# The last stage of an attention, expert and gated-product kernel, put in another order

## The chip, the cores and the metric

The kernel runs on one core of a Trainium2 chip. A core has five engines that run side by side, each through its own list of instructions in order: TensorE (PE in the profile; PEld is its weight load), VectorE (DVE), ScalarE (ACT), GpSimd (POOL) and SyncE (SP), which here only starts DMAs. Matrix products land in PSUM, eight banks of 128 x 512 fp32 numbers; all other data is in SBUF. The metric is the device time of one execution in microseconds: the median of three runs of the kernel before is 660.23 us (657.31 to 660.39).

## The reference

Three stages follow one another. Attention with a local and a global part gives `x` (1536 tokens x 512). Each token then goes to the one expert of eight that a gate picks, `relu(x @ w1[e]) @ w2[e]`, scaled. The last stage is the one that is changed:

```python
def _moe2_ref(x, w_a, w_b, w_out):      # x 1536x512, w_a and w_b 512x1536, w_out 1536x512
    a = x @ w_a
    b = x @ w_b
    return (a * b @ w_out).astype(np.float32)
```

The inputs of the last stage's weights are 64-bit floats, which the kernel turns into 32-bit ones itself.

## The kernel before

**Products in three parts.** A 32-bit number is split into a high part `h` (rounded, type fp32r) and a low part `l = x - h`. Each 128-deep product is three matmuls, high x high, high x low and low x high (`mul`, lines 1104 to 1111, and `out_tile`, lines 1154 to 1173). Every operand therefore costs a cast on ScalarE (`h`) and a subtraction on VectorE or GpSimd (`l`).

**Weights.** `wm` holds 18 tiles of 128 x 1024: numbers 0 to 11 carry, for a block `f` of 128 columns, `w_a` and `w_b`; numbers 12 to 17 carry `w_out`. A half tile `(m, half)` passes through four functions. `cload` (line 847) starts a DMA into one of three buffers `st`. `conv1` is two ScalarE operations, the second in place in `st`. `conv2` is three VectorE operations, clip (line 871), shift (873) and merge (874), and one GpSimd add (876), after which `st` is free. `conv3` is a ScalarE cast (884) and a GpSimd subtraction (885). The result of the add, `tx`, has four buffers.

**Stages.** Eight experts run first (`for k, n in enumerate(CAPS)`, line 917). Each is a first product over eight blocks (`up`) and a second over four (`down`), with background work called from `tick(i)`, i = 0 to 15: 0 to 7 follow the blocks of the first product, 8 to 15 lie in the second. The table `CV` (line 909) sets which conversions ride along. A block `h` of the first product passes ScalarE and VectorE (lines 721 to 726) before the second product can read it. Then comes a conditional block (`tc.If(rare[0] == 1)`, line 979), taken only if an expert has more tokens than planned; with these inputs it is not taken, but every engine passes its branch.

**The last stage.** The tokens are three chunks `c` of 512. For chunk 0 the operands were read and split during the experts (`yT`). For chunks 1 and 2 six DMAs bring them into `acc` behind the branch (line 1246), and `ysp` splits them. Blocks `f` = 0 and 1 are multiplied plainly (`plain`, 48 matmuls for each of the three chunks, lines 1255 to 1262). Blocks 2 to 11 run through `seven(f)`, called a step below: chunks 0 and 1 share seven products instead of eight (`pa`, `pb`, `pc` are its PSUM banks; `T1` to `T4` are sums of weight quarters, made for the next step by `tsum`, four VectorE operations, and split by `tsplit`; `S1` to `S4`, `A11`, `A12`, `A22` are the token side), chunk 2 is multiplied plainly into the banks `ab`. The products `a` and `b` are multiplied and split into `gh` and `gl` (`gate`). After each odd step twelve output tiles (`out_tile`, six matmuls each, three PSUM buffers `o`) become possible; `fill(n)` issues `n` of them. A step holds 66 matmuls and six tiles of six, 102 in all. VectorE adds every tile into `acc` (line 1166).

**What sets the order.** The schedule is written by hand (`tc.manual_schedule()`): each engine runs its instructions in the order in which the calls stand in the code, and semaphores make it wait. So a waiting instruction holds up all that is behind it on its engine.

Of the kernel before, what the change touches and what calls it, by code (L numbers as in the profile page):

```python
# [46 lines left out]
def moe_block_kernel(ctx, tc, qd, kd, vd, kt, vn, nv, wg, wg2, we, wm, out):  # L47
# [819 lines left out]
    def conv2(j):  # L867
        sv, tx = raw64.pop(j), tx32[j]
        h, l, txi = sv[:, :, 1], sv[:, :, 0], tx[:, :].bitcast(I32)

# [446 lines left out]
```

## Time and profile before

| what | value |
|---|---|
| median of three runs | 660.23 us (657.31 to 660.39) |
| profiled execution | 659.8 us, of which the span is 658.1 us |
| TensorE busy | 583.6 us (89%) |
| VectorE busy | 460.0 us (70%) |
| ScalarE busy | 307.1 us (47%) |
| GpSimd busy | 253.5 us (39%) |

The shares are means over stages with different limits. In the last stage the slices of the profile's page show VectorE at 5 to 9 tenths and TensorE between 6 and 9, so the question there is which engine is waited for at each pause of TensorE. Matmuls are pipelined: a 128 x 512 one is shown as 0.39 us long, while the next starts some 0.23 us later, so a stretch is measured from start to start.

### The profile page before, as it was taken

To read this page: it belongs to the slowest core of one execution; us is meant where nothing else is said; L and a number is where in the kernel's file an instruction comes from. 1 tells how busy PE (TensorE), PEld (TensorE's weight loads), DVE (VectorE), ACT (ScalarE), POOL (GpSimd) and SP (SyncE) were. 2 spreads that over 40 slices of the span, in tenths; PEclk is the share of its full clock that TensorE was granted. 3 is DMA by queue.
4 is the path that set the end of the run, shared out by engine and by line. 5 is a ranking of instruction groups with operands and counts; after the bars stand their busy time and mean duration, and the time that the engine had idled before them with its cause. 6 is when DMAs were issued, how large, how long until landed. Compare 5 with 4: busy or idle time off the path is not lost.

```text
span 658.1 us, 9962 instructions
## 1 busy us (share of the span) xinstructions
PE 583.6 (89%) x3395; PEld 491.9 (75%) x3395; DVE 460.0 (70%) x982; ACT 307.1 (47%) x681; POOL 253.5 (39%) x231
## 2 busy tenths in 40 slices
PE   6998994999999998987967998898799799879996
PEld 4786773899999897987745776677587577758784
DVE  6888785877447777771676577695876859587653
ACT  5776772556557766761445333423413332341210
POOL 3001532644354655532225544252433415253215
PEclk9999996899999998998979999899799979989999
DMA  8367515475667977844410112020110202010004
GB/s 284 124 206 278 164 55 166 165 254 197 224 224 228 290 258 219 274 155 139 175 64 32 64 65 85 12 97 30 66 64 33 96 0 97 29 67 0 1 22 170
DMA packets 34431, 85.14 MB, mean 129 GB/s; under 512 B 5792, under 2 KB 12192, under 8 KB 34368
## 3 DMA queue, kind: packets, MB, share of 16 engines
q1 hardware_dynamic: 27456, 71.45, 32.2%
q10 hardware_dynamic: 4752, 6.00, 2.9%
q0 software_dynamic: 2160, 6.91, 2.9%
q8 instruction: 31, 0.51, 0.3%
q14 instruction: 32, 0.26, 0.1%
HBM read 73.25 MB, written 11.10 MB: 128 GB/s over the span
## 4 chain that ended last, share of the span: by engine, by line
DVE 21%; PE 16%; issue 7%; ACT 6%; POOL 2%; POOLq 0%; DVEq 0%; ACTq 0%
DVE tx L873 3%; PE ps_o L1161 3%; PE ps_o L1159 3%; DVE tx L874 3%; PE ps_o L1160 3%; DVE gl L1126 2%; DVE tx L871 2%; DVE tt L1093 2%; ACT tx L862 2%; POOL out L1168 1%; ACT st L864 1%; PE ps_pa L1110 1%; PE ps_pa L1109 1%; PE ps_pa L1111 1%; DVE p L1215 1%
## 5 line engine op out<-in xcount | busy, mean ns | idle before, releaser
L110 POOL TENSOR_TENSOR wl<-st,wh 128x512 fp32r<-128x512 f32 x54 | 70.1, 1319 | 89.6 <-ACT wh L105 80.0
L876 POOL TENSOR_TENSOR tx<-tx,st 128x512 int32<-128x512 int32 x36 | 51.0, 1416 | 125.5 <-DVE tx L874 86.6
L105 ACT CAST wh<-st 128x1024 fp32r<-128x1024 f32 x64 | 67.3, 1054 | 33.0 <-DMA st<-we 32.0
L1159 PE MATMUL ps_o<-wh,gh 128*128 128x512 f32 x144 | 61.6, 427 | 20.6 <-ACT gh L1125 8.9
L885 POOL TENSOR_TENSOR wl<-tx,wh 128x512 fp32r<-128x512 f32 x36 | 50.2, 1408 | 66.2 <-ACT wh L884 66.2
L110 DVE TENSOR_TENSOR wl<-st,wh 128x1024 fp32r<-128x1024 f32 x37 | 52.5, 1418 | 28.7 <-ACT wh L105 28.7
L712 PE MATMUL ps_y<-h,wl 128*128 128x256 f32 (+5 forms) x256 | 69.9, 273 | 0.0
L712 PE MATMUL ps_h<-x,wl 128*128 128x256 f32 (+5 forms) x256 | 69.4, 271 | 0.0
L1161 PE MATMUL ps_o<-wh,gl 128*128 128x512 f32 x144 | 61.4, 426 | 5.7 <-DVE gl L1126 5.7
L1160 PE MATMUL ps_o<-wl,gh 128*128 128x512 f32 x144 | 60.3, 418 | 0.0
L1166 DVE TENSOR_TENSOR acc<-ps_o,acc 128x512 f32<-128x512 f32 x60 | 40.5, 686 | 25.2 <-PE ps_o L1161 24.9
L708 PE MATMUL ps_y<-h,wh 128*128 128x448 f32 (+3 forms) x160 | 53.3, 389 | 4.4 <-DVE h L726 4.1
L511 ACT ACTIVATE pe<-pe,mx 128x256 f32<-128x256 f32 (+1 forms) x96 | 45.9, 481 | 22.0 <-DVE mx L507 22.0
L1159 PEld LDWEIGHTS ps_o<-wh,gh 128*128 128x128 f32 x144 | 29.5, 205 | 32.3 <-ACT gh L1125 10.7
L712 PEld LDWEIGHTS ps_y<-h,wl 128*128 128x128 f32 x256 | 50.2, 196 | 0.0
L712 PEld LDWEIGHTS ps_h<-x,wl 128*128 128x128 f32 x256 | 49.4, 193 | 0.0
L708 PE MATMUL ps_h<-x,wh 128*128 128x448 f32 (+3 forms) x160 | 47.9, 365 | 0.0
L884 ACT CAST wh<-tx 128x512 fp32r<-128x512 f32 x36 | 22.2, 620 | 54.0 <-POOL tx L876 53.7
L1161 PEld LDWEIGHTS ps_o<-wh,gl 128*128 128x128 f32 x144 | 29.4, 204 | 14.6 <-DVE gl L1126 7.4
L507 DVE CUSTOM_DVE_ANT_0 pe<-ps_s,bias 128x256 f32<-128x256 f32 (+1 forms) x96 | 32.8, 398 | 7.7 <-PE ps_s L501 6.6
L708 PEld LDWEIGHTS ps_y<-h,wh 128*128 128x128 f32 x160 | 31.7, 198 | 7.7 <-ACT hs L724 4.5
L1125 ACT CAST gh<-a 128x512 fp32r<-128x512 f32 x16 | 9.9, 620 | 56.8 <-DVE a L1227 42.6
(302 smaller groups left out, 1588.5 us busy)
## 6 DMA issues: line engine op xcount, KB each, us to landing
st<-we SPq DMA_DIRECT2D x63, 512.0 KB, 4.4
st<-wm SPq DMA_DIRECT2D x32, 512.0 KB, 3.4
vc<-vd SPq DMA_DIRECT2D x16, 352.0 KB, 3.9
k<-kd SPq DMA_DIRECT2D x7, 464.0 KB, 5.7
x_dram<-x SPq DMA_DIRECT2D x6, 512.0 KB, 3.8
acc<-y_dram SPq DMA_DIRECT2D x6, 512.0 KB, 6.3
q<-qd SPq DMA_DIRECT2D x7, 384.0 KB, 6.0
st<-wm ACTq DMA_DIRECT2D x4, 512.0 KB, 5.0
```

Source lines behind the costliest of these rows:

```text
L105: A.copy(wh, st)
L110: eng.tensor_tensor(wl[:, r], st[:, r], wh[:, r].bitcast(F32), ALU.subtract)
L507: V.tensor_tensor_reduce(out=pe[:, t_, j, 0:n], in0=ps[:, j, t_, 0:n], in1=bias[2 * p + j][:, b0:b0 + n], op0=ALU.add, op1=ALU.min, scale= ...
L511: A.activation(pe[:, t_, j, 0:n], pe[:, t_, j, 0:n], AF.Exp, bias=mx[:, t_, j:j + 1], scale=-1.0, accum_out=sm[:, t_, j:j + 1])
L708: T.matmul(pt[:, 0:2 * n].rearrange("p (s n) -> p s n", s=2), a, M[:, k], start=(k == 0), stop=False)
L712: T.matmul(pt[:, 0:n], b, M[:, k, 0], start=False, stop=(k == last))
L876: G.tensor_tensor(txi, txi, l, ALU.add)
L885: G.tensor_tensor(wl_, tx, wh.bitcast(F32), ALU.subtract)
L1159: T.matmul(po, gh, wh, start=(i == 0), stop=False)
L1160: T.matmul(po, gh, wl, start=False, stop=False)
L1161: T.matmul(po, gl, wh, start=False, stop=(i == 1))
L1166: V.tensor_tensor(acc[:, m], po, acc[:, m], ALU.add)
```

## The change

Line numbers of the changed kernel differ: lines 871, 873, 874, 876 become 874, 876, 877, 879; lines 884 and 885 become 890 and 891; `tsum` moves to 1115 to 1118, `tsplit`'s subtraction from 1102 to 1125, line 1189 to 1240, lines 1196 and 1197 to 1254 and 1255. The parts:

- `conv2` takes several halves and issues all clips, then all shifts, all merges, all adds.
- In the last expert the conversion of tile 1 moves out of the first product into the second.
- The 48 matmuls of chunk 0 for blocks 0 and 1 (`first`) stand in front of the conditional block, in four PSUM buffers of the experts; the block repeats them at its end if it is taken.
- `a * b` is written over the bank that holds `b` (or the corresponding sum), and `gh` and `gl` are made from PSUM.
- In a step all three conversions of the next weights are issued at its start, their casts and subtractions together later, and the products, tiles and gates are put in another order, different for even and odd `f`.
- The opening of the last stage is reordered, and `fill` takes the chunks in the order 2, 0, 1.

The diff, cut to its core:

```diff
@@ product, up, down: the PSUM buffers they take are now a parameter
+    def product(Ws, M, n, name, top, bg=None, tag=("h", 6)):
...
+        pt = ps.tile([P, 512], F32, tag=tag[0], bufs=tag[1], name=name)
...
@@ conv2: one call for several halves, operation by operation
-    def conv2(j):
-        sv, tx = raw64.pop(j), tx32[j]
-        h, l, txi = sv[:, :, 1], sv[:, :, 0], tx[:, :].bitcast(I32)
-        V.tensor_scalar(tx, tx, LO32, HI32, ALU.max, ALU.min)
-        V.tensor_scalar(txi, txi, 3, 0x3FFFFFF8, ALU.logical_shift_left, ALU.bitwise_and)
-        V.scalar_tensor_tensor(txi, h, -0x40000000, txi, ALU.bitwise_and, ALU.bitwise_or)
-        G.tensor_tensor(txi, txi, l, ALU.add)
+    def conv2(*js):
+        ops = []
+        for j in js:
+            sv, tx = raw64.pop(j), tx32[j]
+            h, l, txi = sv[:, :, 1], sv[:, :, 0], tx[:, :].bitcast(I32)
+            ops.append((
+                lambda tx=tx: V.tensor_scalar(tx, tx, LO32, HI32, ALU.max, ALU.min),
+                lambda t=txi: V.tensor_scalar(t, t, 3, 0x3FFFFFF8, ALU.logical_shift_left, ALU.bitwise_and),
+                lambda t=txi, h=h: V.scalar_tensor_tensor(t, h, -0x40000000, t, ALU.bitwise_and, ALU.bitwise_or),
+                lambda t=txi, l=l: G.tensor_tensor(t, t, l, ALU.add)))
+        for o in zip(*ops):
+            for f in o:
+                f()
@@ the last expert's table of background work
-        (7, 11): [(cload, nc.sync)], (7, 12): [(cload, nc.sync)], (7, 13): [(cload, nc.sync)],
-        (7, 2): [(conv1, (1, 0)), (conv2, (1, 0))], (7, 9): [(conv1, (1, 1)), (conv2, (1, 1))],
+        (7, 8): [(conv1, (1, 0))], (7, 9): [(conv2, (1, 0))], (7, 10): [(conv1, (1, 1))], (7, 11): [(conv2, (1, 1))],
+        (7, 12): [(cload, nc.sync)], (7, 13): [(cload, nc.sync)], (7, 14): [(cload, nc.sync)],
@@ behind the last expert, in front of the conditional block
+    def first():
+        for (f, s_), pt in N0.items():
+            mul(pt, wab(f, s_), yT, True)
     yq.pop(0)()
+    for h in range(2):
+        conv3((1, h))
+    N0 = {(f, s_): ps.tile([P, 512], F32, tag="h", bufs=6, name="ps_n") for f in range(2) for s_ in range(2)}
+    first()
@@ inside the conditional block, at its end (and its up/down take ("x", 2))
+            first()
@@ the gated product is written into PSUM
+    def evict(c, f, pp, h1=(), h2=()):
+        a = tmp("a")
+        A.copy(a, pp[0])
+        run_all(h1)
+        V.tensor_tensor(pp[1], a, pp[1], ALU.mult)
+        low = gate(c, f, pp[1])
+        run_all(h2)
+        low()
...
@@ seven(f), a step; its body is now
+        mul(pa, wab(f, 0, 0, 2), A11, True)
+        A.copy(p1, pa)
+        conv_a()
+        mul(pb, T2, S2, True)
+        V.tensor_tensor(u2, pb, p1, ALU.add)
+        mul(pc, T1, S1, True)
+        mul(pa, wab(f, 0, 2, 4), A12, False, True, True)
+        if f % 2:
+            if jobs:
+                tsum(f + 1)
+            ab2(0)
+        else:
+            fill(2)
+            if jobs:
+                tsum(f + 1)
+            fill(2)
+        conv_b()
+        mul(pb, T3, S3, False, True, True)
+        V.tensor_tensor(u3, pb, p1, ALU.add)
+        V.tensor_tensor(u3, u3, pc, ALU.add)
         if f % 2:
+            low2 = ab2(1)
+            low1 = p4()
+            low2()
+            low0 = p3()
+            low1()
+            low0()
+            for j in nxt:
+                conv1(j)
             both(f // 2)
             fill(6 if f < 11 else 12)
+        else:
+            fill(2)
+            for j in nxt:
+                conv1(j)
+            low1 = p4()
+            low0 = p3()
+            low1()
+            low0()
+            ab2(0)
+            ab2(1)()
     def both(p):
-        items.extend((p, c, t_) for c in (1, 0, 2) for t_ in range(4))
+        items.extend((p, c, t_) for c in (2, 0, 1) for t_ in range(4))
@@ the opening of the last stage
-    plain(0, 0, ("pa", "pb"), [(c12, (12, 0))], [(ysp, X[1, 0], S4, V)])
-    plain(0, 1, ("ab", "ab"), [(ysp, X[1, 1], A22, V)], [(c12, (12, 1)), (conv3, (12, 0))])
...
+    evict(0, 0, (N0[0, 0], N0[0, 1]), [(c12, (12, 0), (12, 1))], [(ysp, X[1, 0], S4, V)])
+    evict(0, 1, (N0[1, 0], N0[1, 1]), [(ysp, X[1, 1], A22, V)], [(conv3, (12, 0)), (ysp, X[2, 0], [y[:, 0:2] for y in Y2], V)])
+    pse.close()
...
+    plain(2, 1, ("pc", "o"), [(ysp, X[1, 1], S1, V), (conv3, (2, 1))], [(ysp, X[1, 0], S3, V), (tsplit, 2)])
+    both(0)
+    fill(2)
+    ysp(X[0, 1], S4, V)
+    c12((13, 0))
+    fill(4)
```

VectorE, in the last expert (`ps_h`, `hs` and `h2` belong to the blocks of the first product, `tx_5120` is a half of tile 1), before:

```order
L725 TENSOR_TENSOR ps_h_5105<-ps_h_5105,hs_5115 128x176
L726 SCALAR_TENSOR_TENSOR h2_5071<-ps_h_5105,h2_5071 128x176
L871 TENSOR_SCALAR tx_5120<-tx_5120 128x512
L873 TENSOR_SCALAR tx_5120<-tx_5120 128x512
L874 SCALAR_TENSOR_TENSOR tx_5120<-st64_4889,tx_5120 128x512
L725 TENSOR_TENSOR ps_h_5127<-ps_h_5127,hs_5137 128x176
L726 SCALAR_TENSOR_TENSOR h2_5071<-ps_h_5127,h2_5071 128x176
L725 TENSOR_TENSOR ps_h_5141<-ps_h_5141,hs_5151 128x176
L726 SCALAR_TENSOR_TENSOR h2_5071<-ps_h_5141,h2_5071 128x176
L725 TENSOR_TENSOR ps_h_5155<-ps_h_5155,hs_5165 128x176
```

and now (`tx_5193` is the same half):

```order
L725 TENSOR_TENSOR ps_h_5162<-ps_h_5162,hs_5172 128x176
L726 SCALAR_TENSOR_TENSOR h2_5071<-ps_h_5162,h2_5071 128x176
L725 TENSOR_TENSOR ps_h_5176<-ps_h_5176,hs_5186 128x176
L726 SCALAR_TENSOR_TENSOR h2_5071<-ps_h_5176,h2_5071 128x176
L874 TENSOR_SCALAR tx_5193<-tx_5193 128x512
L876 TENSOR_SCALAR tx_5193<-tx_5193 128x512
L877 SCALAR_TENSOR_TENSOR tx_5193<-st64_4889,tx_5193 128x512
L734 TENSOR_TENSOR yt_5214<-ps_y_5190,yt_5214 128x176
L874 TENSOR_SCALAR tx_5220<-tx_5220 128x512
L876 TENSOR_SCALAR tx_5220<-tx_5220 128x512
L877 SCALAR_TENSOR_TENSOR tx_5220<-st64_4957,tx_5220 128x512
```

The three conversion operations stood in front of five blocks' operations and now stand behind the last block.

VectorE in the odd step `f` = 5 from the second conversion on (`tx_6710` and `tx_6713` are the halves of tile 6, `tx_6716` one of the output weights, `tt` the sums of `tsum`), before:

```order
L871 TENSOR_SCALAR tx_6713<-tx_6713 128x512
L873 TENSOR_SCALAR tx_6713<-tx_6713 128x512
L874 SCALAR_TENSOR_TENSOR tx_6713<-st64_6560,tx_6713 128x512
L1196 TENSOR_TENSOR u3_6724<-ps_pb_6720,p1_6722 128x512
L1197 TENSOR_TENSOR u3_6724<-u3_6724,ps_pc_6721 128x512
L871 TENSOR_SCALAR tx_6716<-tx_6716 128x512
L873 TENSOR_SCALAR tx_6716<-tx_6716 128x512
L874 SCALAR_TENSOR_TENSOR tx_6716<-st64_6608,tx_6716 128x512
L1092 TENSOR_TENSOR tt_5790<-tx_6713,tx_6710 128x256
L1093 TENSOR_TENSOR tt_5790<-tx_6713,tt_5790 128x256
L1094 TENSOR_TENSOR tt_5790<-tx_6713 128x256
L1095 TENSOR_TENSOR tt_5790<-tx_6710,tt_5790 128x256
```

and now, from the first shift on (the halves are `tx_6700`, `tx_6703` and `tx_6706`):

```order
L876 TENSOR_SCALAR tx_6700<-tx_6700 128x512
L876 TENSOR_SCALAR tx_6703<-tx_6703 128x512
L876 TENSOR_SCALAR tx_6706<-tx_6706 128x512
L877 SCALAR_TENSOR_TENSOR tx_6700<-st64_6602,tx_6700 128x512
L877 SCALAR_TENSOR_TENSOR tx_6703<-st64_6604,tx_6703 128x512
L877 SCALAR_TENSOR_TENSOR tx_6706<-st64_6606,tx_6706 128x512
L1240 TENSOR_TENSOR u2_6769<-ps_pb_6766,p1_6768 128x512
L1115 TENSOR_TENSOR tt_5892<-tx_6703,tx_6700 128x256
L1116 TENSOR_TENSOR tt_5892<-tx_6703,tt_5892 128x256
L1117 TENSOR_TENSOR tt_5892<-tx_6703 128x256
L1118 TENSOR_TENSOR tt_5892<-tx_6700,tt_5892 128x256
L1254 TENSOR_TENSOR u3_6770<-ps_pb_6766,p1_6768 128x512
```

The sums into `u3` stood in front of `tsum` and the third conversion; now they stand behind both.

GpSimd for the same three halves (`wl` are low parts of weights), before:

```order
L876 TENSOR_TENSOR tx_6710<-tx_6710,st64_6554 128x512
L876 TENSOR_TENSOR tx_6713<-tx_6713,st64_6560 128x512
L885 TENSOR_TENSOR wl_6772<-tx_6710,wh_6771 128x512
L885 TENSOR_TENSOR wl_6772<-tx_6713,wh_6771 128x512
L876 TENSOR_TENSOR tx_6716<-tx_6716,st64_6608 128x512
L1102 TENSOR_TENSOR wl_6802<-tt_5790,wh_6801 128x512 x2
L885 TENSOR_TENSOR wl_6850<-tx_6716,wh_6849 128x512
```

and now:

```order
L879 TENSOR_TENSOR tx_6700<-tx_6700,st64_6602 128x512
L879 TENSOR_TENSOR tx_6703<-tx_6703,st64_6604 128x512
L879 TENSOR_TENSOR tx_6706<-tx_6706,st64_6606 128x512
L891 TENSOR_TENSOR wl_6835<-tx_6700,wh_6834 128x512
L891 TENSOR_TENSOR wl_6835<-tx_6703,wh_6834 128x512
L891 TENSOR_TENSOR wl_6841<-tx_6706,wh_6840 128x512
L1125 TENSOR_TENSOR wl_6845<-tt_5892,wh_6844 128x512 x2
```

The third add stood behind two subtractions; now three adds and three subtractions follow one another.

## Rows read from the trace of the kernel before

**Rows 1.** TensorE by stretches: start:end, us, busy (instructions), granted clock, DMA share, GB/s
```profile
291.38:366.62 75.24, 59.26 (x247) 0.89 0.27 90
299.08:304.53 5.45, 5.45 (x42) 1.00 0.78 222
366.62:620.22 253.60, 224.59 (x919) 0.96 0.15 52
620.22:635.30 15.08, 15.08 (x67) 1.00 0.00 0
...
442.40:445.00 2.60, 0.96 (x4) 1.00 0.00 0
466.00:477.00 11.00, 7.35 (x20) 0.69 0.14 49
```

**Rows 2.** Waits of TensorE, steps to the end: engine, line waited for, total, times, longest
```profile
PE ps_o L1159 <- ACT gh L1125: 8.9, 4, 2.2
PE ps_pa L1109 <- ACT p L1187: 7.2, 5, 1.6
PE ps_o L1159 <- DVE acc L1166: 6.5, 4, 1.6
PE ps_o L1161 <- DVE gl L1126: 5.7, 4, 1.4
```

**Rows 3.** Waits of TensorE from the last expert's second product to the first step
```profile
PE ps_pa L1109 <- ACT Y2h L1083: 4.8, 1, 4.8
PE ps_o L1159 <- ACT acc L1164: 4.3, 1, 4.3
PE ps_pa L1109 <- DVEq L979: 3.7, 1, 3.7
PE ps_y L708 <- DVE h L726: 1.8, 2, 1.7
```

**Rows 4.** Timeline, VectorE and GpSimd inside one odd step: start, us, engine, line
```profile
455.64 0.43 DVE L873 TENSOR_SCALAR tx<-tx 128x512 int32<-128x512 int32 x1
...
460.71 2.90 POOL L885 TENSOR_TENSOR wl<-tx,wh 128x512 fp32r<-128x512 f32 x2
...
461.07 1.40 DVE L873 TENSOR_SCALAR tx<-tx 128x512 int32<-128x512 int32 x1
...
462.51 1.66 DVE L874 SCALAR_TENSOR_TENSOR tx<-st,tx 128x512 int32<-128x512 int32 x1
...
467.77 2.53 POOL L1102 TENSOR_TENSOR wl<-tt,wh 128x512 fp32r<-128x512 f32 x2 [2.11 <-ACT wh L1100]
...
467.86 0.68 DVE L1218 TENSOR_TENSOR u<-ps_pc,u 128x512 f32<-128x512 f32 x1
```

**Rows 5.** Groups on VectorE in nine steps: count, busy us, mean ns
```profile
L1126 DVE TENSOR_TENSOR gl<-p,gh 128x512 fp32r<-128x512 f32 x9 | 15.2, 1693 | 0.0
...
L1093 DVE TENSOR_TENSOR tt<-tx,tt 128x256 f32<-128x256 f32 x9 | 12.7, 1411 | 0.3
...
L1126 DVE TENSOR_TENSOR gl<-u,gh 128x512 fp32r<-128x512 f32 x9 | 6.1, 678 | 0.0
...
L1094 DVE TENSOR_TENSOR tt<-tx 128x256 f32<-128x256 f32 x9 | 3.7, 411 | 0.0
```

**Rows 6.** Line 979 (the conditional): ns min/median/max, first and last start
```profile
L979 PEldq EVENT_SEMAPHORE  x2: 51/51/51, 304.7 to 304.9; - x2
...
L979 DVEq EVENT_SEMAPHORE  x2: 21/21/21, 308.2 to 308.3; - x2
```

**Rows 7.** Line 1246 (loads into `acc`): ns min/median/max, first and last start; time to landing
```profile
L1246 SPq DMA_DIRECT2D acc<-y_dram x6: 395/462/525, 308.9 to 311.4; - x6
...
DMA to landing us min/median/max: 3.6/6.3/8.4
```

**Rows 8.** Tile `acc`: the first split made from it, ns min/median/max
```profile
L1083 ACT CAST S4h<-acc x1: 1048/1048/1048, 317.0 to 317.0; 128x1024 fp32r<-128x1024 f32 x1
L1085 DVE TENSOR_TENSOR S4l<-acc,S4h x1: 1227/1227/1227, 318.1 to 318.1; 128x1024 fp32r<-128x1024 f32 x1
```

More of the change, by code (lines that the diff above doesn't have):

```diff
@@ L715, in product, with up @@
         return (pt[:, 0:n], pt[:, n:2 * n]) if two else (pt[:, 0:n],)
-    def up(W, f, X, n, Hm, pool, f0=0):
-        pp = product([[x[:, f * P:(f + 1) * P] for x in W(k)] for k in range(4)], X, n, "ps_h", 255)
+    def up(W, f, X, n, Hm, pool, f0=0, tag=("h", 6)):
+        pp = product([[x[:, f * P:(f + 1) * P] for x in W(k)] for k in range(4)], X, n, "ps_h", 255, None, tag)
         h, l = (Hm[:, f0 + f, j] for j in range(2))
@@ L836, in moe_block_kernel @@
     wstep(V, 2)
-    MW, TW, TX = {}, {}, {}
+    MW, TW = {}, {}
     WO = {f: (12 + (f + 1) // 2, 1 - f % 2) for f in range(2, 11)}
@@ L971, in moe_block_kernel, with mul, wab @@
                 yq.pop(0)()
+    def mul(pt, w, y, start, stop=True, more=False):
+        (wh, wl), (yh, yl) = w, y
+        n = wh.shape[1]
+        for k in range(n):
+            T.matmul(pt, wh[:, k, :], yh[:, k, :], start=start and k == 0, stop=False, skip_group_check=more)
+            T.matmul(pt, wh[:, k, :], yl[:, k, :], start=False, stop=False, skip_group_check=more)
+            T.matmul(pt, wl[:, k, :], yh[:, k, :], start=False, stop=stop and k == n - 1, skip_group_check=more)
+    def wab(f, s_, k0=0, k1=4):
+        return [w[:, :].rearrange("p (s k n) -> p s k n", s=2, k=4)[:, s_, k0:k1] for w in MW[f]]
+    def first():
+        for (f, s_), pt in N0.items():
+            mul(pt, wab(f, s_), yT, True)
     yq.pop(0)()
+    for h in range(2):
+        conv3((1, h))
+    N0 = {(f, s_): ps.tile([P, 512], F32, tag="h", bufs=6, name="ps_n") for f in range(2) for s_ in range(2)}
+    first()
     ep.close()
@@ L1102, in tsplit @@
             G.tensor_tensor(wl[:, a:a + 512], tv[:, a:a + 512], wh[:, a:a + 512].bitcast(F32), ALU.subtract)
-    def mul(pt, w, y, start, stop=True, more=False):
-        (wh, wl), (yh, yl) = w, y
-        n = wh.shape[1]
-        for k in range(n):
-            T.matmul(pt, wh[:, k, :], yh[:, k, :], start=start and k == 0, stop=False, skip_group_check=more)
-            T.matmul(pt, wh[:, k, :], yl[:, k, :], start=False, stop=False, skip_group_check=more)
-            T.matmul(pt, wl[:, k, :], yh[:, k, :], start=False, stop=stop and k == n - 1, skip_group_check=more)
     def bank(tag, bufs=1):
@@ L1126, in gate @@
         return lambda: V.tensor_tensor(gl, a, gh[:, :].bitcast(F32), ALU.subtract)
+    def evict(c, f, pp, h1=(), h2=()):
[6 more added lines that the diff above has]
+        low()
     def plain(c, f, tags, h1=(), h2=()):
-        pp = []
-        for s_ in range(2):
-            pt = bank(tags[s_], 2 if tags[s_] == "ab" else 1)
+        pp = [bank(t_, {"ab": 2, "o": 3}.get(t_, 1)) for t_ in tags]
+        for s_, pt in enumerate(pp):
             if c == 1:
@@ L1136, in plain @@
             else:
-                mul(pt, wab(f, s_), Y2 if c else yT, True)
-            pp.append(pt)
-            if s_ == 0:
-                a = tmp("a")
-                A.copy(a, pt)
-                run_all(h1)
-        V.tensor_tensor(a, a, pp[1], ALU.mult)
-        low = gate(c, f, a)
-        run_all(h2)
-        low()
+                mul(pt, wab(f, s_), Y2, True)
+        evict(c, f, pp, h1, h2)
     def run_all(fs):
```

117 lines of the change are left out of this document (50 added, 67 removed).

## The prediction

> **What bounds the kernel now.** I read the shares first, then TensorE by stretches, then TensorE's waits, then the timeline of VectorE and GpSimd in one step.
>
> The stretches [rows 1] tell what the stage would take if TensorE never paused. The last step's 66 matmuls ran from 620.22 to 635.30 without a pause (the count of 67 holds one from in front): 15.08/66 = 0.2285 us each. A step with its six tiles is 102 matmuls, 102 x 0.2285 = 23.3 us. The nine steps from 366.62 to 620.22 took 253.6 us, so 253.6 - 9 x 23.3 = 43.9 us are pauses and slow clock. The stretch in front, from the start of the last expert's second product (291.38) to the first step (366.62), took 75.2 us. Its matmuls are 32 pairs in the expert, at 5.45/20 = 0.2725 us a pair (the count of 42 includes the edges), 8.7 us, and 180 at 0.2285, 41.1 us: 49.8 us, so 25.4 us are lost there. Together 69 us of the span could go at the very most.
>
> Who is waited for in the steps [rows 2]: the high and low parts of the gated product, 2.2 and 1.4 us in four odd steps; the copy `p`, held up behind six conversions on ScalarE, 1.6 us each; VectorE's adds of tiles in four even steps, 1.6 us each. That is 28.3 us. [...] In front of the steps the waits are for the branch, for the split of chunk 2, for a copy of the first tiles, and for a block of the last expert [rows 3].
>
> Why VectorE is late: its operations stretch while GpSimd works. A shift takes 0.43 us alone and 1.40 us beside GpSimd, and the merge behind it 1.66, one VectorE operation for each GpSimd one [rows 4]. An operation with one operand in PSUM runs through at 0.68 us beside GpSimd [rows 4]. The low part from two SBUF operands takes 1.69 us beside GpSimd and 0.68 us otherwise, an operation of `tsum` 1.41 against 0.41 [rows 5].
>
> **The change part by part.**
>
> *Last expert.* The conversion leaves VectorE's list in front of the blocks, so the wait of 1.7 us for `h` [rows 3] and the slow clock behind it go: the pairs ran to 304.5 [rows 1], 304.5 - 291.4 - 8.7 = 4.4 us. The conversion's new place lies behind the last block, where only copies out of PSUM follow, with banks to spare; if that cover failed, the loss would be the old 4.4 us. Bounds 0 and 4.4; I take 4.4, since nothing is left in front of the blocks.
>
> *Products in front of the branch.* 48 matmuls, 48 x 0.2285 = 11.0 us, now follow the expert at once: 291.4 + 8.7 + 11.0 = 311.1. The wait of 3.7 us for VectorE's branch is covered, since VectorE needs the time up to 308.2 beside TensorE's 304.7 [rows 6]. But the loads into `acc` stand behind every engine's branch, TensorE's too. They started 0.6 us behind VectorE's semaphore [rows 6, 7]; now they start about 311.9. The first landing takes 3.6 us at the least [rows 7], so 315.5; the cast of S4 takes 1.05 and the subtraction 1.23 us [rows 8]. TensorE's next matmul needs the cast (316.6), its second the subtraction (317.8): 6.5 us of waiting, where before it went on with chunk 0. Behind it I put 2.0 us of slow clock, half way between 3.9 (the 15.6 us over four odd steps' pairs of waits) and nothing (behind a wait of 1.6 us). Then 96 matmuls, 21.9 us: 341.5.
>
> *First tiles.* These now start with chunk 2, whose second block has just been multiplied. VectorE has 22 operations between S4 and that product, 1.2 us for a double-width one, 0.65 for others, 23 us, and I add some 6 us for six GpSimd operations beside them (1.0 us each, as in rows 5): free about 346. Then product, cast, split of S3 and the low part, 0.7 + 0.6 + 2.3 + 0.7 = 4.3 us: 350.3. TensorE would be there at 342.9 (six matmuls); 7.4 us of waiting, again 2 us of clock. With six tiles (8.2 us) the first step starts at 341.5 + 7.4 + 2 + 8.2 = 359.1, against 366.6: 7.5 us gained, of which 4.4 from the expert.
>
> *Even steps.* At the start VectorE runs nine conversion operations (6 x 0.43 us [rows 4] and three merges at 0.7, as other operations of that size [rows 5], 4.7 us), the third merge behind the first add. GpSimd then has three adds and three subtractions in a row, 1.45 us each (2.90 for two [rows 4]), and all four operations of `tsum` wait for one each: instead of 1.41 + 3 x 0.4 = 2.6 us they take some 5 us, to 13.9 us of the step. Four of the six tiles and T3 (so I call the product with that sum, and T4 alike) hide nearly all; the sixth tile needs the third's add and comes 1.0 us late. 24.3 us. Were this cover gone, T4 would wait too, about 2.5 us more. The copy `p` is free of conversions, which now lie beside T4 or the tiles: its wait of 1.6 us goes.
>
> *Odd steps.* VectorE begins 2.2 us late, behind the even step's last product, cast and low part (0.25 + 0.7 + 0.6 + 0.65). Conversions to 8.0, `u2` to 8.6: T3 starts at 8.8 instead of 8.2, 0.6 us late. The second add ends at 9.3, `tsum` begins, meets the third add and three subtractions, 4 x 1.45, and ends at 15.1; `u3` is ready at 15.8. T4 may not overwrite its bank before that, and TensorE stands there at 12.9: 3.0 us of waiting. Behind T4 come `u2`, three low parts, then six tiles; the low parts read PSUM and are not held up [rows 4, 5], the first tile needs `gl` of chunk 2 at 19.3, which is there. So 23.3 + 3.6, and of slow clock I take 1.6: the wait of 3.0 lies between 1.6 us, which cost nothing, and 2.2 + 1.4, which cost 3.9 at most. 28.5 us.
>
> *The gate in PSUM.* Its cost in VectorE time is bounded by two rows: 0.68 us with a PSUM operand [rows 4], 0.68 without [rows 5]. I take no difference. [...]
>
> *Last step.* No weights follow and no GpSimd work lies beside it; it had no pause and keeps its time, as do the last twelve tiles and stores.
>
> *Sum.* Five even steps 5 x 24.3 = 121.5, four odd 4 x 28.5 = 114.0: 235.5 against 253.6, 18.1 us gained. With 7.5 in front 25.6: 659.8 (the profiled execution: 658.1 of span and 1.7 around it) - 25.6 = 634.2. The median of the runs lies 0.4 us above the profiled execution, which I neglect. **634 us.** Its own range is 622 to 648: T4's wait between 0.6 and 5 us.
>
> **The rivals.**
>
> *TensorE becomes the bound.* If only one operation of `tsum` meets GpSimd, as before [rows 5], T4 waits at most 0.3 us and no clock is lost: even 23.6, odd 23.9, 5 x 23.6 + 4 x 23.9 = 213.6, 40 us gained, and 8 in front: 612. For it: VectorE's load is 17.4 us a step when nothing holds it (conversions 4.7, `tsum` 1.6, 17 others at 0.65). Against it: six GpSimd operations in a row, ready one behind the other.
>
> *The gain goes into the clock.* If each wait, also that of 1.0 us in even steps, ends in a slow stretch of 3.3 us, a step takes 27.6 or 30.2: 5 x 27.6 + 4 x 30.2 = 258.8, 5.2 us more than now, and in front 2.6 us of the gain go, 4.9 remain: 660, no change. Against it: no wait of 1.6 us did so.
>
> *Slower: VectorE behind GpSimd.* The place is the list of VectorE in every step. If all eight GpSimd operations of a step each hold one VectorE operation for 1.0 us, 17.4 becomes 25.4 us, and with T4 and the tiles waiting in turn some 4 us come on top in each step, clock included: 29.5 x 9 = 265.5, 12 us more; in front the late loads eat the gain but for 4: 668. It decides from a mean step of 253.6/9 + 7.5/9 = 29.0 us on. For it: the first tile's and T4's waits stand one behind the other in the same lists.
>
> **How the numbers follow.** What a measurement of this kernel can tell from no change is about 0.5%, 656.9 to 663.5. Forecast 0.50, TensorE bound 0.27, clock 0.10 (of it 0.07 within 0.5%, 0.03 below), slower 0.13 (0.11 beyond 0.5%, 0.02 just under). Faster 0.50 + 0.27 + 0.03 + 0.02 = 0.82, same 0.07, slower 0.11. The range reaches from the fast side of the TensorE case (605) to 656; some 0.05 lie below and 0.15 above.
>
> **What would show it.** Right: no wait of TensorE for `h` in the last expert; a wait of 5 to 8 us for S4h behind the branch; one for `gl` at the first tile; in odd steps a wait of T4 for `u3`, and all four operations of `tsum` near 1.4 us; none for `p`, and the low parts at 0.68 us. Wrong: steps of 23.5 us both (TensorE bound), or TensorE waiting for tiles' adds in even steps by more than 3 us, or a granted clock under 0.9 throughout the steps (the slower cases).

## The result and the profile after

The changed kernel takes 629.45 us (median of 4 runs, 628.93 to 633.74), the kernel before 659.95 us beside it (657.31 to 660.39): ratio 0.9562, 95% interval 0.9521 to 0.9604, 30.5 us less. The profiled execution of the changed kernel is 633.74 us with a span of 632.0 us, 26.1 us less than the one of before.

The two profiled executions can't be subtracted as they stand. But for one conversion, the work in front of the last expert's second product is unchanged, and yet that product starts at 291.38 us before, at 293.17 us after, and at 288.1 to 295.6 us in the runs below; and behind TensorE's last matmul 5.8 us passed before, 8.8 us after, 6.3 to 8.0 us in the runs below. So I measure from the start of that product to the end of the last matmul: 360.9 us before, 330.1 us after, 30.8 us less, which is what the medians say. Of these 7.5 us lie in front of the first step and 23.4 us in the nine steps.

TensorE by stretches in the profile after (start:end, us, busy and instructions, granted clock, DMA share, GB/s), beside [rows 1]:

```profile
293.17:360.90 67.73, 56.23 (x247) 0.87 0.32 108
...
313.20:327.00 13.80, 6.32 (x16) 0.63 0.84 304
...
360.90:591.14 230.24, 219.23 (x920) 0.97 0.18 58
385.60:413.48 27.88, 25.36 (x103) 0.94 0.18 57
...
464.87:488.39 23.52, 23.52 (x104) 1.00 0.20 68
```

The stretch in front takes 67.73 us instead of 75.24 and the nine steps 230.24 instead of 253.60. The last two rows are one odd and one even step: the even one is at TensorE's bound (23.3 us for 102 matmuls), the odd one 4.6 us above. The even steps took 25.4 us before, the odd ones 30.9 to 32.3.

TensorE's waits after, from the last expert to the end (line waited for, total us, times, longest), beside [rows 2, 3]:

```profile
PE ps_pb L982 <- DVE u L1254: 10.1, 4, 2.5
PE ps_pc L982 <- ACT S4h L1106: 7.0, 1, 7.0
PE ps_o L1173 <- DVE gl L1137: 2.1, 1, 2.1
PE ps_o L1171 <- ACT gh L1136: 1.9, 1, 1.9
PE ps_pa L982 <- ACT p L1237: 0.9, 1, 0.9
PE ps_pc L983 <- DVE S4l L1108: 0.5, 1, 0.5
```

Gone are the waits for `gh`, `gl` and the tiles' adds in the steps [rows 2] and for `h` in the expert [rows 3]; of those for `p` one of 0.9 us is left, in the first step. New is one wait per odd step, T4 for `u3` (tile `u`, L1254), and those for the two parts of S4 behind the branch. The lines for `gl` and `gh` above are the first tiles, in front of the steps. What stands in front of `u3` in an odd step (VectorE, then GpSimd; start, us), beside [rows 4, 5]:

```profile
445.58 1.52 DVE L1115 TENSOR_TENSOR tt<-tx 128x256 f32<-128x256 f32 x1 [1.87 <-POOL tx L879]
447.14 1.40 DVE L1116 TENSOR_TENSOR tt<-tx,tt 128x256 f32<-128x256 f32 x1
448.46 1.50 DVE L1117 TENSOR_TENSOR tt<-tx 128x256 f32<-128x256 f32 x1
449.89 1.48 DVE L1118 TENSOR_TENSOR tt<-tx,tt 128x256 f32<-128x256 f32 x1
451.29 0.68 DVE L1254 TENSOR_TENSOR u<-ps_pb,p 128x512 f32<-128x512 f32 x1
...
446.76 4.33 POOL L891 TENSOR_TENSOR wl<-tx,wh 128x512 fp32r<-128x512 f32 x3
```

All four operations of `tsum` take 1.4 to 1.5 us beside GpSimd's third addition and three subtractions, 0.41 us without [rows 5].

### The profile page after: what moved, and what is told of

Its sections match the earlier page's. It is cut to its first block, busy times and chain, and to the rows that moved or that the text cites. A ratio compares the mean times of both kernels' runs of the same rounds, so it can differ in the third digit from the quotient of the medians.

```text
span 632.0 us, 9974 instructions
## 1 busy us (share of the span) xinstructions
PE 576.4 (91%) x3395; PEld 488.6 (77%) x3395; DVE 448.4 (71%) x984; ACT 307.9 (49%) x681; POOL 254.9 (40%) x227
## 4 chain that ended last, share of the span: by engine, by line
PE 33%; DVE 9%; issue 4%; ACT 2%; POOL 1%; DMA 1%; POOLq 0%; SPq 0%; DVEq 0%; ACTq 0%
PE ps_o L1173 5%; PE ps_o L1171 5%; PE ps_o L1172 5%; PE ps_pb L982 2%; PE ps_pb L984 2%; PE ps_pb L983 2%; PE ps_ab L984 2%; PE ps_ab L983 2%; PE ps_ab L982 2%; PE ps_pc L983 2%; PE ps_pc L982 1%; PE ps_pc L984 1%; DVE tx L877 1%; DVE tt L1115 1%; DVE tt L1117 1%
## 5 line engine op out<-in xcount | busy, mean ns | idle before, releaser
L879 POOL TENSOR_TENSOR tx<-tx,st 128x512 int32<-128x512 int32 x36 | 57.9, 1632 | 133.7 <-issue 101.4
L105 ACT CAST wh<-st 128x1024 fp32r<-128x1024 f32 x64 | 67.3, 1053 | 32.2 <-DMA st<-we 31.1
L110 DVE TENSOR_TENSOR wl<-st,wh 128x1024 fp32r<-128x1024 f32 x37 | 53.0, 1432 | 25.8 <-ACT wh L105 25.4
L891 POOL TENSOR_TENSOR wl<-tx,wh 128x512 fp32r<-128x512 f32 x36 | 52.5, 1480 | 21.3 <-ACT wh L890 15.7
L1173 PE MATMUL ps_o<-wh,gl 128*128 128x512 f32 x144 | 58.2, 404 | 2.1 <-DVE gl L1137 2.1
L1171 PE MATMUL ps_o<-wh,gh 128*128 128x512 f32 x144 | 58.0, 403 | 1.9 <-ACT gh L1136 1.9
L1172 PE MATMUL ps_o<-wl,gh 128*128 128x512 f32 x144 | 57.8, 401 | 0.0
L708 PE MATMUL ps_y<-h,wh 128*128 128x448 f32 (+3 forms) x160 | 50.4, 373 | 3.4 <-DVE h L726 3.1
L712 PEld LDWEIGHTS ps_y<-h,wl 128*128 128x128 f32 x256 | 48.5, 189 | 0.0
L1171 PEld LDWEIGHTS ps_o<-wh,gh 128*128 128x128 f32 x144 | 27.7, 192 | 9.6 <-ACT gh L1136 2.4
L1173 PEld LDWEIGHTS ps_o<-wh,gl 128*128 128x128 f32 x144 | 27.7, 192 | 9.3 <-DVE gl L1137 2.5
L726 DVE SCALAR_TENSOR_TENSOR h<-ps_h,h 128x256 fp32r<-128x256 f32 (+5 forms) x64 | 24.9, 393 | 12.8 <-ACT h L721 11.4
L501 PE MATMUL ps_s<-k,q 64*128 64x256 f32 (+1 forms) x192 | 27.8, 412 | 5.6 <-DMA q<-qd 5.6
```

The lines of the kernel that those rows point to most:

```text
L105: A.copy(wh, st)
L110: eng.tensor_tensor(wl[:, r], st[:, r], wh[:, r].bitcast(F32), ALU.subtract)
L708: T.matmul(pt[:, 0:2 * n].rearrange("p (s n) -> p s n", s=2), a, M[:, k], start=(k == 0), stop=False)
L712: T.matmul(pt[:, 0:n], b, M[:, k, 0], start=False, stop=(k == last))
L879: lambda t=txi, l=l: G.tensor_tensor(t, t, l, ALU.add)))
L891: G.tensor_tensor(wl_, tx, wh.bitcast(F32), ALU.subtract)
```

## The experiments

All are edits of the changed kernel. "Front" is the stretch from the last expert's second product to the first step, "stage" that from the same point to the last matmul, both from the trace; odd and even are typical steps behind the first. The changed kernel, e2, e3 and e9 have the same code in front of the first step, and their fronts are 67.7, 68.3, 67.3 and 68.8 us: a difference of less than about 1.5 us there tells nothing.

| kernel | median us | ratio to before (95%) | front | odd | even | stage |
|---|---|---|---|---|---|---|
| before | 659.95 | | 75.2 | 31.6 | 25.4 | 360.9 |
| changed | 629.45 | 0.9562 (0.9521-0.9604) | 67.7 | 27.9 | 23.5 | 330.1 |
| e1 expert early | 630.81 | 0.9565 (0.9513-0.9617) | 71.6 | 27.8 | 23.5 | 333.5 |
| e2 subs behind | 616.21 | 0.9358 (0.9305-0.9412) | 68.3 | 24.6 | 23.5 | 317.8 |
| e3 tsum behind | 615.95 | 0.9356 (0.9302-0.9411) | 67.3 | 24.9 | 23.5 | 317.8 |
| e4 S4 first | 629.74 | 0.9563 (0.9503-0.9623) | 69.8 | 26.9-27.9 | 23.5 | 330.8 |
| e5 half in front | 624.17 | 0.9462 (0.9425-0.9499) | 62.3 | 27.7 | 23.5 | 324.2 |
| e6 all behind | 626.40 | 0.9490 (0.9451-0.9528) | 65.8 | 26.9-27.9 | 23.5 | 327.4 |
| e7 ungrouped | 631.72 | 0.9565 (0.9525-0.9605) | 69.1 | 27.4 | 24.1 | 331.8 |
| e8 gate in SBUF | 636.12 | 0.9643 (0.9606-0.9680) | 74.9 | 27.9 | 23.5 | 337.0 |
| e9 odd old | 619.46 | 0.9387 (0.9355-0.9418) | 68.8 | 25.5 | 23.5 | 321.7 |
| e10 even old | 640.25 | 0.9708 (0.9673-0.9743) | 63.5 | 30.4 | 24.0 | 340.1 |
| e11 odd old, SBUF | 637.35 | 0.9635 (0.9604-0.9667) | 74.8 | 27.7 | 23.5 | 336.4 |
| c2 all together | 607.11 | 0.9205 (0.9172-0.9238) | 56.1 | 23.6 | 23.8 | 307.4 |

**The odd step's wait (e2, e3).** e2 moves the casts and GpSimd's subtractions (those of the conversion and of the split of the sums) behind T4, e3 moves `tsum` behind `u3`, each in odd steps alone. In short:

```diff
 e2, odd steps
-        conv_b()              # in front of T3
...
             low1 = p4()
+            conv_b()
             low2()
 e3, odd steps
-            tsum(f + 1)       # in front of ab2(0)
...
             V.tensor_tensor(u3, u3, pc, ALU.add)
+            tsum(f + 1)
             low2 = ab2(1)
+            tsplit(f + 1)     # out of conv_b
```

> In odd steps the casts and the GpSimd subtractions of the conversion come behind T4 instead of in front of T3; the four operations of tsum stay in front of u3. Theory A (each operation of tsum is held up by one GpSimd subtraction): tsum meets only the third add, its operations take 0.4 to 0.8 us but for one, T4's wait of 2.5 us and the 1.8 us of slow clock behind it go in four odd steps, 4 x 4.3 = 17 us; the low parts read PSUM and are not held; 612 us, up to 617 if the first tiles or the next step's A11 wait. Rival B (tsum is late or long by itself, for the add or by its place in the list): the wait stays at 1.5 us or more, 625 us or above.

> In odd steps the four operations of tsum stand behind u3, their split behind the gated product of chunk 2; the GpSimd subtractions stay where they are. Theories A and B: u3 meets at most one subtraction (1.4 us instead of 0.7), T4's wait of 2.5 us goes or falls under 0.5, 612 to 617 us. Rival C (the lateness only moves): the product of chunk 2 or the split of the sums is late instead, TensorE waits for a gl at the tiles or for T2 in the next step, 624 us or above.

The same place of VectorE's timeline in e2, with `tsum` where it was:

```profile
437.85 1.51 DVE L1115 TENSOR_TENSOR tt<-tx 128x256 f32<-128x256 f32 x1 [1.85 <-POOL tx L879]
439.40 0.42 DVE L1116 TENSOR_TENSOR tt<-tx,tt 128x256 f32<-128x256 f32 x1
439.74 0.42 DVE L1117 TENSOR_TENSOR tt<-tx 128x256 f32<-128x256 f32 x1
440.08 0.41 DVE L1118 TENSOR_TENSOR tt<-tx,tt 128x256 f32<-128x256 f32 x1
440.41 0.68 DVE L1254 TENSOR_TENSOR u<-ps_pb,p 128x512 f32<-128x512 f32 x1
```

Only the first operation still meets an addition; the other three take 0.42 us, T4's wait is gone, and 3.3 us of an odd step with it. Theory A holds and rival B falls: `tsum` stands at its old place in VectorE's list, and what left its side are the casts and GpSimd's subtractions. The medians fell by 13.2 and 13.5 us, the stage by 12.3 in both, not by 17. TensorE's new waits in the steps, e2 and then e3:

```profile
PE ps_o L1171 <- DVE acc L1178: 3.6, 4, 0.9
...
PE ps_o L1173 <- DVE gl L1137: 2.3, 4, 0.6
```

In e2 each odd step waits 0.9 us for a tile's add. In e3 each waits 0.6 us for `gl` at the tiles, and some 0.8 us more (24.9 us against the 23.5 of an even step) stand in no row of this table; rival C (the lateness only moves) is worth no more than that.

**The branch (e4, e5, e6).** e4 puts the split of S4 ahead of the conversion of (12,*); e5 leaves the first block's 24 matmuls in front of the branch and puts the other 24 behind it; e6 puts all 48 behind it.

```diff
 e4
-evict(0, 0, ..., [(c12, (12, 0), (12, 1))], [(ysp, X[1, 0], S4, V)])
+evict(0, 0, ..., [(ysp, X[1, 0], S4, V), (c12, (12, 0), (12, 1))], [])
 e5 (e6: no first() in front, the whole of it behind)
-    first()
+    first(0)
 ...
     with tc.If(rare[0] == 1):
 ...
+    first(1)              # behind the conditional's body
```

> Behind the branch the split of S4 stands in front of the conversion of (12,0) and (12,1) on ScalarE and VectorE. Theory A (ScalarE's list, not the landing, sets TensorE's wait of 7.0 us for S4h): the cast starts when the first load lands, some 3.7 us behind 313.8, at 317.5 instead of 319.1, the wait falls to 5.4 us: 627.8 us, less what the later conversion costs at the first tiles (up to 2 us). Rival B (the landing sets it): the wait stays at 7 us, 629.4 us or above.

> Only the first block's 24 matmuls stand in front of the branch, the second block's 24 behind it. Theory A (the loads start when the last engine is past the branch, and TensorE's 11.3 us in front of it hold up loads, first eviction and conversions alike): TensorE is past the branch 5.6 us earlier, the loads start at about 308 instead of 313.8, their landing and ScalarE's list run beside the other 24 matmuls, the wait of 7.0 us for S4h falls to 1 or 2 us and the slow clock behind it shrinks: 621 to 623 us. Rival B (the wait only moves to the first tiles, because VectorE's list sets them): waits of 1.9 and 2.1 us there grow to 8 us or more in sum, 627 us or above.

> All 48 matmuls stand behind the branch. Theory A (moving them in front was worth nothing by itself, since the loads moved back with TensorE): TensorE idles some 4.8 us until VectorE is past the branch, the wait for S4h falls to 0 to 1 us: 626 to 631 us, no difference from 629.4. Theory B (the forecast's sum, by which the front gained 3.1 us beside the expert's 4.4): 632 us or above.

In the changed kernel the conditional (L1003) reads, engine by engine (ns min/median/max, first and last start):

```profile
L1003 DVEq EVENT_SEMAPHORE  x2: 21/21/21, 306.6 to 306.7; - x2
L1003 PEldq EVENT_SEMAPHORE  x2: 51/51/51, 313.2 to 313.4; - x2
...
L1003 DVEq COMPARE_BRANCH  x1: 63/63/63, 302.5 to 302.5; - x1
...
L1003 PEldq COMPARE_BRANCH  x1: 3339/3339/3339, 308.8 to 308.8; - x1
```

VectorE is past it at 306.7, TensorE only with its last matmul at 313.2. ScalarE waits for that before its first copy, and the loads into `acc` (L1287) start behind it too:

```profile
L1287 SPq DMA_DIRECT2D acc<-y_dram x6: 395/462/530, 313.8 to 316.3; - x6
...
DMA to landing us min/median/max: 3.7/4.6/5.4
```

```profile
313.31 0.59 ACT L1142 COPY a<-ps_n 128x512 f32<-128x512 f32 x1 [9.84 <-PEq L1003]
...
318.59 0.59 ACT L1136 CAST gh<-ps_n 128x512 fp32r<-128x512 f32 x1 [2.49 <-DVE ps_n L1144]
319.08 1.05 ACT L1106 CAST S4h<-acc 128x1024 fp32r<-128x1024 f32 x1
```

By the shortest of these times to landing the first load is there 3.7 us behind 313.8, at 317.5; the cast of S4 starts at 319.1, behind a cast that waited for VectorE's conversions. In e4 the wait for S4h falls to 5.4 us as theory A has it, but A22h, now behind the conversions, is waited for 3.0 us, and nothing is gained. In e5 the waits there are 0.7 and 0.8 us and the front is 5.4 us shorter: theory A, less some 1 us that comes back at the first tiles (2.5 us for `gh`, 2.7 for `gl`). TensorE's wait for S4h in e5, and its waits at the branch in e6:

```profile
PE ps_pc L982 <- ACT S4h L1107: 0.7, 1, 0.7
...
PE ps_n L983 <- DVEq L1002: 3.2, 1, 3.2
...
PE ps_n L982 <- ACTq L1002: 1.5, 1, 1.5
```

e6 has TensorE idle 4.7 us at the branch and no wait for S4h, and is 1.9 us shorter in front, 3.0 by the median, little more than the noise of either. So putting all 48 in front of the branch gained nothing and may have lost a little; of the three splits tried, half of them is the best.

**The expert (e1).** The conversion of (1,0) and (1,1) goes back to its old places, and with it the three starts of loads beside it (not shown).

```diff
-(7, 8): [(conv1, (1, 0))], (7, 9): [(conv2, (1, 0))], (7, 10): [(conv1, (1, 1))], (7, 11): [(conv2, (1, 1))],
+(7, 2): [(conv1, (1, 0)), (conv2, (1, 0))], (7, 9): [(conv1, (1, 1)), (conv2, (1, 1))],
```

> The conversion of the blocks (1,0) and (1,1) goes back among the last expert's blocks; all else as in the changed kernel (629.4 us median). Theory A (the forecast's term): the wait of 1.7 us for h and the slow clock behind it come back, 4.4 us on the path, since TensorE is the last engine at the branch: 633.9 us, and a wait for h of 1.5 to 1.9 us in the expert. Rival: the front is set by what follows the branch, so the delay is absorbed: 629 to 630 us.

TensorE's wait in the expert's second product:

```profile
PE ps_y L708 <- DVE h L726: 1.6, 3, 1.3
```

The wait for `h` came back, the expert's product took 13.3 us instead of 8.75, the front 3.9 us more: in the trace the delay is as theory A has it, and it isn't absorbed. The median rose by only 1.4 us, to 630.81, between theory A's 633.9 and the rival's 630, and the two intervals (3 us each way) can't tell these apart: what the move is worth in the time of a run is not shown.

**The gate in PSUM and the grouping (e8, e7).** e8 writes the gated products to SBUF as before (four places of the kind shown), e7 converts half by half.

```diff
 e8
-        V.tensor_tensor(pp[1], a, pp[1], ALU.mult)
-        low = gate(c, f, pp[1])
+        V.tensor_tensor(a, a, pp[1], ALU.mult)
+        low = gate(c, f, a)
 e7
-        for o in zip(*ops):
+        for o in ops:
```

> The gated products are written to SBUF again. Theory A (the low parts no longer lie beside GpSimd work, because the conversions moved): they take 0.68 us from SBUF too, a few meet a subtraction at 1.4 to 1.7 us: 629 to 632 us. Rival B (the PSUM operand is what freed the low parts): several per step take 1.4 us or more, TensorE waits for gl at the tiles again, 634 us or above.

> The conversions of a step go half by half again (clip, shift, merge, addition of one half, then of the next), in the new order of the step. Theory A (the additions of the first two halves each hold up one or two VectorE operations, 1 us each, and T3 waits for u2 behind them in odd steps): 0.5 to 1.5 us more in odd steps, nothing in even ones, which have tiles to hide it: 631 to 636 us. Rival B (grouping is what made the steps short): every step 1.5 us or more longer, 640 us or above. Rival C (grouping is worth nothing): 629 to 630 us.

e8 is 6.7 us slower, but neither theory has the place: the steps are as long as before the edit and all 7.2 us lie in front. Two rows of VectorE and one of ScalarE there:

```profile
338.96 1.80 DVE L1137 TENSOR_TENSOR gl<-a,gh 128x512 fp32r<-128x512 f32 x1
...
346.11 1.75 DVE L1137 TENSOR_TENSOR gl<-a,gh 128x512 fp32r<-128x512 f32 x1
```

```profile
340.84 0.59 ACT L1142 COPY a<-ps_pa 128x512 f32<-128x512 f32 x1 [2.28 <-DVE gl L1137]
```

Three of the six low parts meet GpSimd and take 1.75 to 1.80 us instead of 0.68, and four times ScalarE's copy into the one buffer `a` must wait 2.0 to 2.3 us for the low part that still reads it; with the product in PSUM `a` is free as soon as it is multiplied. How the 7.2 us divide between the two is not shown. e7 shows rival C for the steps: T3 waits 1.1 us for `u2` in odd steps, as theory A said, but T4's wait falls from 2.5 to 1.7, and odd and even steps go from 27.9 and 23.5 to 27.4 and 24.1, no difference in sum (230.6 us for nine, against 230.2). Its 2.3 us in the median are inside the intervals, and the 1.4 us that the trace has in front are inside the spread of the fronts.

**The order of the steps (e9, e10, e11).** e9 gives the odd steps their old order, e10 the even ones; e11 is e9 with the gate in SBUF. The grouping of the conversions stays in all three. The old order needs chunk 1's tiles first: e9 has them so for the pairs 1 to 4, e10 for 0 to 4. In short:

```diff
 e9 (f odd) and e10 (f even), in seven(f)
+        A11; copy p1; T2; u2; conv2(*jobs); T1; A12; T3; u3
+        conv3(jobs); [even: fill(2)]; conv2(wo); tsum; ab(0); tsplit; copy a
+        low1 = p4(); low0 = p3(); low1(); low0()
+        [even: fill(4)]; ab2(1)(); conv3(wo); conv1(nxt); [odd: both, fill(6)]
```

> The odd steps issue their work in the old order (chunk 2's products behind T4 and in front of the tiles, chunk 1's tiles first, conversions of the second kind in front of tsum and the third behind it), with the gate in PSUM, the expert, the front and the even steps as in the changed kernel. Theory A (the order of the odd step itself is what shortened it from 31.6 to 27.9 us): 4 x 3.7 = 15 us more, 644 us, with waits for gl or gh at the tiles. Rival B (the low parts from PSUM are enough, since they are not held up by GpSimd): no wait at the tiles, odd steps of 24 to 28 us, 629 us or below.

> The even steps issue their work in the old order (T3 in front of the tiles, four tiles in front of chunk 2's last product, conversions of the second kind for the third block behind T3), the odd steps stay new; chunk 1's tiles come first for every pair but the last, which the old order needs, so the first tiles of the stage don't wait for chunk 2 either. Theory A (the order of the even step shortened it from 25.4 to 23.5 us): even steps of 25.4 us, 5 x 1.9 = 9.5 us more, less some 5 us at the first tiles: 634 us, 639 without that. Rival B (only the conversion in front of the copy `p` mattered, or the low parts from PSUM): even steps of 23.5 to 24 us, 625 to 630 us.

> The old order of the odd steps as in the run e9, and the gated products in SBUF as in the run e8: what the odd step of the kernel before has, in the surroundings of the changed kernel. Theory A (the products in PSUM and the new order are two cures of one wait, the low parts held up by GpSimd; e9 kept one, e8 the other, here both are gone): the low parts beside the split of the sums take 1.4 to 1.7 us, TensorE waits for gl and gh some 2.2 and 1.4 us in each odd step, these take 29 to 31.6 us instead of 25.5: 14 to 24 us more, and 7 us in front: 640 to 650 us. Rival B (the old odd order was freed by something else, the even step in front of it or the copy of p): odd steps stay under 27 us, 626 to 632 us.

e9 is the surprise: with the old order the odd step takes 25.5 us, 2.4 less than in the new order, and the median is 10.0 us lower. Rival B holds, but for 1.2 us of waiting (`gh` 0.7, `gl` 0.5) that is left at the tiles. In e9 the low parts lie beside the split of the sums on GpSimd and aren't held up:

```profile
400.52 0.68 DVE L1137 TENSOR_TENSOR gl<-ps_pb,gh 128x512 fp32r<-128x512 f32 x1
401.27 0.69 DVE L1137 TENSOR_TENSOR gl<-ps_pa,gh 128x512 fp32r<-128x512 f32 x1
```

```profile
399.12 2.52 POOL L1125 TENSOR_TENSOR wl<-tt,wh 128x512 fp32r<-128x512 f32 x2 [2.12 <-ACT wh L1123]
```

In e11, from SBUF at the same place, the first of them is:

```profile
408.73 1.67 DVE L1137 TENSOR_TENSOR gl<-p,gh 128x512 fp32r<-128x512 f32 x1
...
410.32 0.68 DVE L1137 TENSOR_TENSOR gl<-u,gh 128x512 fp32r<-128x512 f32 x1
```

and the odd step takes 27.7 us, 2.2 more (1.0 us of waiting, and TensorE busy 25.5 us instead of 24.3 at a granted clock of 0.94 instead of 1.00). So PSUM cures the wait for the held-up low parts in the old order, and in the new order, where they lie elsewhere, it makes no difference to the steps (e8): two cures of one wait, as theory A has it. Its size was wrong: steps of 27.7 and not 29 to 31.6 us, and 637.35 us lies between its 640 to 650 and rival B's 626 to 632. The other 3.9 us of the old odd step come from neither. In the traces some 3 us of them are waits, 1.6 us for `p` and 1.4 us for `gh` (2.2 before, 0.8 in e11), the rest is busy time of TensorE at slow clock (26.8 us at 0.89 in the step of 32.1 us, 25.5 us at 0.94 in e11). What remains for them is the even step in front, with all that is new there, and the grouping. For `p` e10 shows the place. By its ranges e10 is neither theory's: the even steps take 24.0 us, as rival B has it, and the front gains 4.2 us, but the odd steps behind them rise to 30.4, and 640.25 us is above theory A's 634 to 639:

```profile
PE ps_pb L982 <- DVE u L1299: 2.5, 1, 2.5
PE ps_pa L982 <- ACT p L1282: 1.6, 1, 1.6
PE ps_o L1173 <- DVE gl L1137: 1.2, 1, 1.2
PE ps_o L1171 <- ACT gh L1136: 0.6, 1, 0.6
```

These are TensorE's waits in one such odd step. The copy `p` waits again behind six conversions on ScalarE, which the old even step issues at its end, and chunk 1's tiles, first in e10, wait for a low part that is made behind chunk 2's. What else than the order took the even step from 25.4 to 24.0 us is open; without the grouping it is 24.1 (e7).

**All together (c2).** Half of the first products in front of the branch (e5), the casts and subtractions behind the last gated product (one product later than in e2), and in front of the steps the first pair's tiles beginning with chunk 1, with the splits S1, S2, S4 among them and the conversion of (13,0) in the product before. In short, without the lines of e5 and of the tiles' order:

```diff
-            low0 = p3()
+            low0 = p3(); conv_b()
...
-    both(0); fill(2); ysp(X[0, 1], S4, V); c12((13, 0)); fill(4)
+    both(0); fill(2); ysp(S1); fill(2); ysp(S2); ssum(X[0, 1]); ysp(S4); fill(2)
```

> Together: half of the first products in front of the branch; in odd steps the casts and subtractions of the conversion behind the last gated product; in front of the steps the splits S1, S2 and S4 among the first six tiles, and the first pair's tiles begin with chunk 1. If the terms add up: odd steps of 23.6 us (4 x 4.3 = 17 us less), 5.4 us less around the branch, 4 us of waits and 3 us of slow clock less at the first tiles: 600 us. If the splits, now later, hold up T2 or the tiles' copies: waits for S2l or acc of 3 us or more, 604 to 610 us.

607.11 us, 22.3 us less than the changed kernel. TensorE by stretches, the front, the first step, and the other eight:

```profile
289.03:345.08 56.05, 51.73 (x247) 1.00 0.41 139
345.08:374.91 29.83, 26.41 (x103) 0.89 0.16 54
374.91:564.33 189.42, 189.37 (x818) 1.00 0.18 59
```

The eight steps run without a pause, 23.7 us each. The first step takes 29.8 us: `p` waits 3.4 us behind the conversions that crowd ScalarE there, and slow clock follows (0.74 granted from 349 to 362 us). These 6 us are most of what lies between 600 and 607.

## Why the prediction was right, and where it wasn't

**The total.** 634 us forecast, 629.45 measured. The profiled executions differ by 26.1 us against the 25.6 of the sum, but that agreement is partly chance: the stage gained 30.8 us, 1.8 us were lost ahead of it and 3.0 us behind its last matmul. Of the signs that I had named all came, but that the first tile waited for `gh` (1.9 us) as well as for `gl`, and that `p` was waited for once.

**Odd steps** (28.5 us forecast, 27.9 measured). The mechanism is as forecast: four operations of `tsum` at 1.4 to 1.5 us, T4 waiting for `u3`, slow clock behind it (0.94 granted over the step). The wait was 2.5 us, not 3.0. I had the third merge held up by the first addition and T3 0.6 us late behind it; the three merges took 1.89 us in all, and it was the addition that was held up:

```profile
441.22 1.89 DVE L877 SCALAR_TENSOR_TENSOR tx<-st,tx 128x512 int32<-128x512 int32 x3
...
442.03 2.25 POOL L879 TENSOR_TENSOR tx<-tx,st 128x512 int32<-128x512 int32 x1 [11.69 <-issue]
```

So the nine conversions took 4.1 us, T3 was on time, and `u3` came 0.8 us earlier in the step than summed. e2 shows the cause of the wait by taking it away.

**Even steps** (24.3 forecast, 23.5 measured, the first of them 24.7). The sixth tile was never late. I had all four operations of `tsum` held up, some 5 us, to 13.9 us of the step; in the step from 464.87 us on they take 0.76, 1.40, 1.52 and 0.41 and end at 13.1 us of the step. With the odd steps' 0.6 us this is the 5.3 us by which the steps came out shorter than the sum.

**The front** (7.5 us gained in both) is right by cancellation, that is by luck. The expert's 4.4 us is confirmed in e1's trace (4.6 in the product, 3.9 in the front), not by its median. For S4h I forecast 6.5 us of waiting and 2.0 of slow clock and got 7.5 and 2.9; at the first tiles I forecast 7.4 and 2 and got 4.0 and 3.2: seen from the stage's start TensorE came there 2.1 us later than summed (52.2 against 50.1) and VectorE's low part 1.2 us earlier. (VectorE's list in front of that product has 28 operations, nine of them double-width, not 22; the 23 us fit the 28.) For S4h a step failed: I had the landing set the cast, and it was ScalarE's list, because ScalarE's first copy too waited until TensorE was past the branch (9.84 us); with the split of S4 first the wait is 5.4 us (e4). I had counted TensorE's branch for the loads alone.

**Slow clock.** The terms for it (2.0 and 2 us in front, 1.6 in an odd step) go back to the 15.6 us that the waits leave of the 43.9 (43.9 - 28.3). That all of these were slow clock was an estimate of mine, and no run shows such a term by itself; by the busy time in [rows 1] TensorE spent 224.6 - 9 x 23.3 = 14.9 us more than its bound there. In the changed kernel its busy time is 1.8 us longer in the odd step than in the even one (25.36 us at 0.94, 23.52 at 1.00); in front, where 2.9 and 3.2 us came out, 0.63 was granted from 313.2 to 327.0 us and 0.70 from 345.8 to 357.0.

**The gate in PSUM** is the step that failed in kind: "I take no difference". In the steps as changed that holds; with the odd steps in their old order it is worth 2.2 us in each (e9 against e11). In front it is worth 7.2 us (e8), by low parts that GpSimd would hold up (1.75 to 1.80 us there instead of 0.68) and by the buffer `a` (copies that wait 2.0 to 2.3 us); I had weighed the duration of the operation and not who holds which buffer. On the duration it was right: in the steps the means of the low parts are 0.684 to 0.692 us from PSUM and the same in e8 from SBUF.

**What the sum never asked** is whether each part pays by itself. The new order of the odd steps doesn't (e9: 2.4 us a step better without, once the gate is in PSUM), and of the 48 products in front of the branch no gain shows (e6: 1.9 us better without, little more than the noise). The rival in which TensorE becomes the bound, 612 us, is not what the change did; e2 and e3 came near it, and c2 went past it.

## What to carry over

Where two engines slow each other down, count for each operation in the waiting list what the other engine runs in the same moment, and try first to move the shorter list: here three additions and three subtractions on one side met four small operations on the path (1.4 to 1.5 us each instead of 0.41). When a change cures a wait in two ways at once, undo each alone; the one that isn't needed may cost more than it gives. Work moved in front of a conditional can hold up other engines behind it until its own engine is through, as here ScalarE's first copy (9.84 us of waiting) and the loads (from 313.8 us on, TensorE through at 313.2), so try how much of it covers the others' passage; here half was better than all or nothing.

## What the runs showed of the hardware

An operation of VectorE that reads SBUF alone was held up by GpSimd one for one (0.41 to 1.4 us in the changed kernel, 0.68 to 1.67 in e11 and to 1.80 in e8); with one input in PSUM it took 0.68 us beside the same work (e9 against e11). When VectorE's merge had begun first, it was GpSimd's addition that took longer (2.25 us in the changed kernel). At the untaken conditional VectorE spent 4.1 us from its compare (302.5) to the first semaphore behind it (306.6), 3.7 in e8, 4.1 in e7 and 5.2 us in e5; TensorE's compare took 3.3 us behind its 48 matmuls. TensorE's clock did not answer to the length of a pause alone: with T4's wait of 2.5 us the odd steps of the changed kernel were granted 0.94, those of e10, with waits of 1.6, 2.5, 0.6 and 1.2 us, 1.00; why is open.
